# Attention and MLP in one kernel: another order of the pieces, and DMA transposes of exp(C) from batch 2 on

## The chip, the cores and the metric

The kernel runs on one core of one Trainium2 chip. The metric is the device time of a run in microseconds, and less is better. TensorE is PE, VectorE is DVE, ScalarE is ACT, GpSimd is POOL and SyncE is SP. PEld is PE's loading of weights.

## The reference

The program is a Nystrom attention followed by a layer with silu. It has 8 batches, 8 heads, 576 positions and a head size of 64. The landmarks are means over 18 positions, 32 of them for each head.

```python
q_lm = q.reshape(B, H, m, S // m, D).mean(axis=3)      # m = 32
k_lm = k.reshape(B, H, m, S // m, D).mean(axis=3)
A = sm(q, k_lm); Bm = sm(q_lm, k_lm); C = sm(q_lm, k)  # sm: scaled softmax
Z = Bm.T / (norm1(Bm) * norminf(Bm) + 1e-06)
for _ in range(6):
    Z = 2 * Z - Z @ Bm @ Z
attn = A @ Z @ C @ v
x = attn.transpose(0, 2, 1, 3).reshape(B * S, H * D)   # 4608 x 512
h = x @ w_in                                           # 512 x 2048
out = (h * sigmoid(h)) @ w_out                         # 2048 x 512
```

## The kernel before, in words

All work is written as some 1,540 small pieces. A piece has a name, an engine that may do it (sometimes one of two), a duration that the author assumed, the pieces it depends on, a priority, and the PSUM banks it takes. A planner at the top of the file (class Plan) runs through time with these assumed durations and gives every engine that is free the ready piece of lowest rank. The table ORDER adds a shift to the priority of named pieces (`shift, o.ready = ORDER.get(o.name, (0.0, 0.0))`, L87); its second number holds a piece back until a model time. The result is a fixed list for each engine. On the chip every engine works through its list in that order and waits where a piece's inputs or its buffer aren't ready. So a piece that waits holds up all that stands behind it on its engine.

The name of a piece ends in its batch. The ones that matter here:

- ld1, ld0 and ldv0 to ldv2 load k, q and v of a batch (POOL's DMA queue, with a cast to bf16). wi.. and wo.. load the weights of the two layers. The buffers qk, qT, v, ct, ce and lm have two copies, which even and odd batches use in turn.
- tr and trc (batches 0 and 1) transpose k and q on PE and copy them to qT. From batch 2 on, four DMA transposes on SP do this: xt10 and xt11 for k (head groups 0 and 1), xt00 and xt01 for q (L587).
- lra, lrb, lrc and lrd on DVE add up the landmarks from qT. lra1 takes both groups of k and lra0 both groups of q. ltr1 and ltr0 are PE matmuls with the matrix `fold` that finish them, and lmT copies them out.
- sb, pb, csb, f0, ns and nsd are the softmax of Bm and the iteration for Z: a chain that goes between PE and DVE.
- C and A are the scores. Cx and Ax are their exponentials on ACT (into ce and et). S, Ln, Rs and etn divide A by its sums. exp(C) has to be transposed. Before the change batches below NCT = 4 do that with six PE transposes for each head group (ctm, L825) and one copy out of PSUM (ctc). Later batches do it with one DMA transpose on SP (ct, L837). cv multiplies with v, and wc, zt and m with mc make the matrix m = Z C v w_in.
- h0 to h15, hx0 and hx8 multiply A with m on PE. g0 to g15, gx0 and gx8 apply silu on ACT, into gm and gx. These steps need another ACT table than exp does, and a table load stands at each change.
- The last product is done for pairs of 128-position blocks with seven half-size products instead of eight. ss0 to ss3 on DVE make the sums of blocks of gm. p1 to p7 are the products on PE, 8 matmuls each. c1, u2, c5, c11, c22, c12 and c21 bring them to the output buffer ost (four copies, used in turn) on ACT or DVE, and os stores it through SP's queue. A name such as p1@5120 has the batch in its hundreds (batch 1, second pair). The first pair of all is done plainly (o0 to o3 at 5000 and 5001, and oc).

Transfers of different kinds are kept apart by extra waits. The transposes of q and k of batch b wait until ldv1 of that batch has landed (L582). The loads of batch b + 1 wait for one transpose of batch b, which is the third that the code creates, xt00:

```python
gate = last[b - 1]["xts"][-2:-1] if b > NPE else []     # L1122, NPE = 2
if b - 2 >= NCT:
    gate = gate + last[b - 2]["cts"][:1]
load_qk(b, 100.0 * b - 150, p["qk_read"], gate)
load_v(b, 100.0 * b - 149, [p["cv"]], gate)
```

The code creates the transposes in the order xt10, xt11, xt00, xt01. The order in which SP issues them is the planner's.

PE also has filler matmuls (on the zero tile zer) in the first 45 us, where the planner sees it idle.

## Time and profile before

| | us |
|---|---|
| median of 3 runs | 259.06 (258.79 to 259.65) |
| profiled execution | 259.06 |
| its span | 257.3 |
| PE busy | 241.2 (94%) |
| ACT busy | 180.7 (70%) |
| DVE busy | 171.8 (67%) |
| PE transposes of exp(C), 48 | 3.6 (mean 219 ns) |
| fillers, 95 | 15.9 (mean 299 ns) |
| DMA transposes on SP | 24 of q and k, 8 of exp(C) |

Busy time is the union of an engine's instructions. Matmuls overlap on PE, so a mean of 219 ns for a transpose doesn't say how far apart two of them start. The time of a DMA is in two parts: how long SP or POOL is taken up by issuing it, and how long it is from there until it has landed.

### The profile page before, as it was taken

What the parts mean: (1) busy time and instruction counts of PE and PEld (TensorE: products, weight loads), DVE (VectorE), ACT (ScalarE), POOL (GpSimd) and SP (SyncE); (2) the same over time, 40 slices, a digit from 0 to 9 for tenths busy, and PEclk for the clock granted to TensorE, in tenths of its full rate; (3) what the DMA queues carried; (4) which work ended last, traced back from release to release, by engine and by line L of the source; (5) the groups of instructions that cost most, each with busy time, mean ns of one, the idle gap of its engine ahead of it and who ended that gap; (6) DMA issues with size and microseconds to landing.
All of it is one profiled execution on the core that took longest, in us unless ns stands there. A gap on an engine that the chain in (4) does not pass through costs nothing.

```text
span 257.3 us, 7005 instructions
## 1 busy us (share of the span) xinstructions
PE 241.2 (94%) x2737; PEld 169.6 (66%) x2737; DVE 171.8 (67%) x433; ACT 180.7 (70%) x428; POOL 37.8 (15%) x64
## 2 busy tenths in 40 slices
PE   7999998999979789999979999999999999999990
PEld 5875655646758445567866655788785585788870
DVE  2378736597958776939979769199995654157520
ACT  2697799689852899997449989678679957721210
POOL 8446621004004003100310040000000000000000
PEclk9999999999999999999999999999999999999997
DMA  5999999999999998996796989974341203033332
GB/s 96 212 195 201 203 207 208 202 154 179 216 179 139 234 171 149 204 175 148 131 225 157 137 156 222 194 164 111 77 105 32 54 3 82 0 85 82 85 103 61
DMA packets 57201, 36.90 MB, mean 143 GB/s; under 512 B 38112, under 2 KB 48608, under 8 KB 57168
## 3 DMA queue, kind: packets, MB, share of 16 engines
q0 software_dynamic: 15296, 18.42, 43.2%
q1 hardware_dynamic: 41536, 17.74, 32.8%
q8 instruction: 21, 0.34, 0.6%
q10 hardware_dynamic: 336, 0.30, 0.4%
q14 instruction: 12, 0.10, 0.1%
HBM read 36.70 MB, written 9.44 MB: 179 GB/s over the span
## 4 chain that ended last, share of the span: by engine, by line
issue 40%; PE 30%; DMA 13%; ACT 4%; SPq 4%; DVE 4%; POOL 3%; POOLq 0%; DVEq 0%; ACTq 0%
PE ps L388 30%; DMA v<-in_v_dram 5%; DMA qT<-qk 3%; DMA w_in_sb<-in_moe_w_in_dram 3%; ACT gm L937 2%; DMA out_dram<-ost 2%; SPq L587 2%; SPq L1002 2%; DVE m L400 1%; POOL qk L446 1%; POOL qk L440 1%; PE ps L825 1%; POOL v L453 1%; DVE st L735 1%; DVE red L623 1%
## 5 line engine op out<-in xcount | busy, mean ns | idle before, releaser
L388 PE MATMUL ps<-etn,m 128*128 128x512 bf16 (+1 forms) x512 | 69.6, 286 | 0.7 <-DVE m L400 0.7
L937 ACT ACTIVATE gm<-ps 128x512 f16<-128x512 f32 x128 | 66.1, 682 | 3.0 <-PE ps L388 2.9
L388 PEld LDWEIGHTS <-gm 128*128 128x128 f16 x512 | 48.4, 98 | 12.7 <-issue 4.5
L388 PE MATMUL ps<-w_out_sb,gm 128*128 128x256 f16 (+1 forms) x392 | 53.9, 281 | 0.9 <-ACT et L765 0.8
L398 ACT COPY ost<-ps 128x256 f32<-128x256 f32 (+1 forms) x59 | 22.5, 386 | 41.2 <-PE ps L388 32.7
L388 PEld LDWEIGHTS <-m 128*128 128x128 bf16 x512 | 31.9, 98 | 26.2 <-issue 5.4
L388 PEld LDWEIGHTS <-ss 128*128 128x128 f16 x408 | 39.5, 98 | 6.9 <-issue 0.2
L1060 DVE TENSOR_TENSOR ost<-ost,ps 128x256 f32<-128x256 f32 x51 | 21.3, 419 | 25.5 <-PE ps L388 10.2
L388 PE MATMUL ps<-wt,ss 128*128 128x256 f16 x272 | 33.9, 273 | 0.0
L735 DVE SCALAR_TENSOR_TENSOR st<-st,ps 128x320 bf16<-128x320 bf16 (+3 forms) x54 | 21.7, 407 | 10.9 <-PE ps L388 10.6
L400 DVE CAST m<-ps 128x512 bf16<-128x512 f32 x32 | 20.9, 687 | 4.1 <-PE ps L388 3.4
L398 ACT CAST m<-ps 128x512 bf16<-128x512 f32 x32 | 17.6, 617 | 2.9 <-PE ps L388 2.8
L453 POOL DMA_DIRECT2D v<-in_v_dram x24 | 14.0, 591 | 26.1 <-PE ps L388 22.0
L388 PE MATMUL ps<-w_out_sb,ss 128*128 128x256 f16 x136 | 17.6, 272 | 0.0
L388 PE MATMUL ps<-zer 128*128 128x256 bf16 x95 | 15.9, 299 | 1.1 <-DVE zer L480 1.1
L446 POOL DMA_DIRECT2D qk<-in_k_dram x7 | 5.0, 716 | 77.1 <-DMA qT<-qk 56.6
L810 ACT ACTIVATE ce<-ps 128x288 bf16<-128x288 f32 x32 | 12.7, 412 | 4.9 <-PE ps L388 4.9
L388 PE MATMUL ps<-wt,gm 128*128 128x256 f16 x120 | 15.6, 273 | 0.0
L1002 POOL DMA_DIRECT2D out_dram<-ost x1 | 0.5, 527 | 97.1 <-DVE ost L1060 97.1
L388 PE MATMUL ps<-st 128*128 128x160 bf16 (+1 forms) x96 | 14.6, 225 | 0.1
L400 DVE COPY ost<-ps 128x256 f32<-128x256 f32 (+1 forms) x11 | 4.9, 448 | 12.2 <-PE ps L388 12.1
L765 ACT ACTIVATE et<-ps 128x288 bf16<-128x288 f32 x32 | 10.8, 418 | 2.5 <-PE ps L388 2.5
(91 smaller groups left out, 331.3 us busy)
## 6 DMA issues: line engine op xcount, KB each, us to landing
out_dram<-ost SPq DMA_DIRECT2D x137, 64.0 KB, 2.1
v<-in_v_dram POOLq DMA_DIRECT2D x24, 192.0 KB, 11.7
qk<-in_k_dram POOLq DMA_DIRECT2D x7, 576.0 KB, 6.2
qk<-in_q_dram POOLq DMA_DIRECT2D x7, 576.0 KB, 9.0
w_out_sb<-in_moe_w_out_dram POOLq DMA_DIRECT2D x4, 512.0 KB, 10.5
w_in_sb<-in_moe_w_in_dram POOLq DMA_DIRECT2D x4, 256.0 KB, 9.3
w_in_sb<-in_moe_w_in_dram POOLq DMA_DIRECT2D x8, 128.0 KB, 7.5
qk<-in_k_dram POOLq DMA_DIRECT2D x2, 288.0 KB, 4.9
```

The source lines that it names most:

```text
L388: nc.tensor.matmul(out=out_ap, lhsT=lhsT, rhs=rhs, start=start, stop=stop, skip_group_check=True)
L398: nc.scalar.copy(out=out, in_=in_)
L400: nc.vector.tensor_copy(out=out, in_=in_)
L446: lambda e, t=t, src=src: nc.gpsimd.dma_start(out=qk_r[b % 2][:, t].rearrange("p g j d -> p g (j d)"), in_=src[b].rearrange("(g h) (l j) d ...
L453: lambda e, a=a: nc.gpsimd.dma_start(out=v_r[b % 2][a * L:(a + 1) * L, :, :], in_=v[b].rearrange("h (l a x) d -> a l h (x d)", l=L, a=VA)[ ...
L587: lambda e, t=t, g=g: nc.sync.dma_start_transpose(out=qT[:, t, g], in_=qk[:, t, g].rearrange("p j d -> p (j d)")),
L735: nc.vector.scalar_tensor_tensor(out=s2[:, g0:g1, lo:SW], in0=s[:, g0:g1, lo:SW], scalar=2.0, in1=ps[:, 0:NG * SW].rearrange("p (g x) -> p ...
L765: lambda e, g=g, et=et, c=c: nc.scalar.activation(out=et[:, c], in_=bank(me["A"], 2 * g + c)[:, 0:HS], func=AF.Exp, scale=sc / J),
L810: nc.scalar.activation(out=ce[:, :, 0:VP].rearrange("p (i c) (a l) -> p c a i l", c=2, a=VA)[:, c], in_=bank(me["C"], 2 * g + c)[:, 0:HS]. ...
L937: lambda e, dc=dc, cell=cell: nc.scalar.activation(out=gm[:, dc, :], in_=bank(cell["o"]), func=AF.Silu),
L1002: {"SP": nc.sync, "ACT": nc.scalar, "POOL": nc.gpsimd}[e].dma_start(out=out[b * S:(b + 1) * S, cols].rearrange("(l j) n -> j l n", j=J)[j] ...
L1060: nc.vector.tensor_tensor(out=out_, in0=x, in1=y, op=OP.add)
```

## The change

NCT becomes 2, so batches 2 and 3 also transpose exp(C) by DMA on SP. By L1123 the loads of batches 4 and 5 then wait for the first such transpose of the batch two before as well. The table ORDER is another one, with 77 entries in place of 46. The first loads are written as a list LOADS with one priority each, and load_qk can load k or q alone; the list names the loads in the sequence they had.

```diff
 ORDER = {
-    "ld11.0": (-7.7871, 0), "lms006.0": (45.257, 0), "nsd11.0": (-1.7367, 0),
...
-    "n1.6": (-1615.8, 0), "Ln10.6": (-887.04, 0), "h6.6": (115.44, 0), "p2@5740.0": (1.5405, 0),
+    "ld00.0": (-5.0016, 0), "tr014.0": (-121.13, 0), "stf0.0": (177.85, 0), "ns40.0": (105.91, 0),
...
+    "xt00.2": (-7.9428, 0),
+    "xt01.2": (-1.9866, 0), "ldv1.3": (-3099.2, 0), "S01.2": (2357.7, 0), "etn0.2": (3457.6, 0),
...
+    "C.3": (0.55052, 79.781),
...
+    "p3@5740.0": (334.88, 0),
 }
...
-    NCT = 4
+    NCT = 2
     XLAG = 3.0
+    LOADS = "k1 q1 v0 w0 w1 w2 w3 o0 o1 o2 o3 v1".split()
...
-    def load_qk(b, prio, deps=(), after=()):
-        for t, src in ((1, k), (0, q)):
+    def load_qk(b, prio, deps=(), after=(), ts=(1, 0)):
+        for t in ts:
+            src = k if t else q
...
-    load_qk(1, -95)
-    load_v(0, -90)
-    for f in range(4):
-        load_w_in(f, -80 + f)
-    for c in range(4):
-        load_w_out(c, -50 + c)
-    load_v(1, -40)
+    for i, x in enumerate(LOADS):
+        p, n = -95 + i, int(x[1])
+        {"k": lambda: load_qk(n, p, ts=(1,)), "q": lambda: load_qk(n, p, ts=(0,)),
+         "v": lambda: load_v(n, p), "w": lambda: load_w_in(n, p),
+         "o": lambda: load_w_out(n, p)}[x[0]]()
```

What the new table does to the lists can be read by putting the two programs' instructions side by side. PE has 2,700 matmuls in place of 2,737: 24 PE transposes fewer and 82 fillers in place of 95. SP has four more DMA transposes of exp(C). On SP the parts that stand otherwise, up to batch 3:

```
before: os@5000 xt10.2 xt11.2 xt00.2 xt01.2 os@5001 os@5020 xt10.3 xt11.3 os@5021 xt00.3 xt01.3 os@5100
after:  os@5000 os@5001 xt00.2 xt01.2 xt10.2 xt11.2 os@5020 os@5021 xt10.3 xt11.3 xt00.3 xt01.3 ct0.2 ct1.2
```

On POOL's queue, for batches 2 and 3:

```
before: ld1.2 ld0.2 ldv0.2 ldv1.2 ldv2.2 ldv1.3 ld1.3 ld0.3 ldv0.3 ldv2.3
after:  ld1.2 ld0.2 ldv1.2 ldv2.2 ldv1.3 ld1.3 ld0.3 ldv0.3 ldv2.3 ldv0.2
```

On PE, around the landmarks and scores of batch 2:

```
before: ... h13.1 ltr1.2 h14.1 h15.1 p6@5020 ltr0.2 hx8.1 p1@5100 sb.2 p7@5020 p2@5100 C.2 p4@5020 p5@5100 A.2
after:  ... h15.1 ltr1.2 hx8.1 h4.1 h10.1 ltr0.2 p1@5100 p1@5120 sb.2 p5@5100 C.2 p6@5100 p6@5120 A.2
```

From batch 4 on, SP takes a batch's transposes in these orders: xt01 xt00 xt10 xt11 (batch 4), xt00 xt01 xt10 xt11 (batch 5), xt00 then ct0.5 and ct1.5 and then xt10 xt01 xt11 (batch 6), xt01 xt00 xt10 xt11 (batch 7). Before, all were xt10 xt11 xt00 xt01.

## The prediction

> **What bounds the kernel now.** I read the page's busy times, the table of 10 us windows, the waits of PE, then the SP, POOL and ACT timelines between 50 and 75 us. Piece names are those of the code (kind, tensor and head group, batch); a piece is found in the timeline by its tiles and place in order.

> ```profile
> span 257.3 us, 7005 instructions
> PE 241.2 (94%) x2737; PEld 169.6 (66%) x2737; DVE 171.8 (67%) x433; ACT 180.7 (70%) x428; POOL 37.8 (15%) x64
> ```

> ```profile
> 70.00:80.00 10.00, 8.22 (x99) 6.97 (x97) 6.83 (x17) 4.74 (x12) 0.03 (x1) 1.00 1.11 173
> 80.00:90.00 10.00, 8.40 (x124) 6.05 (x121) 8.15 (x27) 6.40 (x23) 3.12 (x5) 1.00 1.02 199
> ...
> 150.00:160.00 10.00, 10.00 (x89) 5.41 (x87) 8.73 (x19) 9.27 (x21) 3.14 (x5) 1.00 0.95 172
> ```

> PE is the bound: 94% of the span, and full in most windows after 30 us. So PE work removed, or a PE wait added, reaches the end nearly one for one. The first 30 us are held by the loads instead. What idles PE in the middle is little:

> ```profile
> PE ps L388 <- ACT ct L398: 1.7, 1, 1.7
> PE ps L388 <- ACT lmT L398: 1.4, 1, 1.4
> ```

> The first is at 71.9 us. ACT stood 2.2 us before c1@5120, whose ost buffer still had a store in flight; the ct copy behind it kept a PSUM bank. The second, at 129.9 us, is the same kind: c5@5300 waits for a store, and lmT0.5 stands behind it.

> The transfers decide those stores, and the rest of this prediction:

> ```profile
> 51.03 6.74 SPq L587 DMA_TRANSPOSE qT<-qk  x4
> 57.87 8.51 SPq L1002 DMA_DIRECT2D out_dram<-ost  x8
> 66.55 5.93 SPq L587 DMA_TRANSPOSE qT<-qk  x2
> ```
> ```profile
> 58.89 0.58 POOL L453 DMA_DIRECT2D v<-in_v_dram  x1 [17.61 <-PE ps L388]
> 59.46 0.71 POOL L446 DMA_DIRECT2D qk<-in_k_dram  x1
> 60.16 0.72 POOL L446 DMA_DIRECT2D qk<-in_q_dram  x1
> 60.88 1.18 POOL L453 DMA_DIRECT2D v<-in_v_dram  x2
> ```

> SP transposes batch 2 with four DMA transposes from 51.03 us; the qT view gives them 3.3 to 3.7 us to landing. Batch 3's loads start at 58.89, about 0.6 us after xt00.2, the third of the four, landed (54.94 + 3.4 = 58.3); the code gates them on that one. By the time these loads move data, all four are through. For the two transposes at 66.55 and 68.70, issued while these loads ran, the same view answers:

> ```profile
> DMA to landing us min/median/max: 5.8/6.4/7.0
> ```

> and the second took 3.8 us to issue instead of 1.3. In 64 to 66 us the DMA engines carry 214 GB/s at a share over 1: full. A transpose that meets loads lands about when the loads are done (the last landed at 72.5).

> [...] SP's transposes and stores slow down when POOL's loads run (3.4 to 7.0 us); what share a transpose keeps, no row shows alone. [...] Here that is 12 transposes in 0.83 us and copies of 0.56 (DVE) or 0.83 us (ACT).

> **The change, part by part.**

> (a) PE transposes out. For batches 2 and 3, 24 matmuls: the block of 12 at 87.56 us lasts 0.83 us, less the 0.22 us of one, over 11 steps, 55 ns each: **-1.3 us** of PE. Three DVE copies (1.7 us) and one ACT copy (0.8) go too.

> (b) DMA in their place: ct0 and ct1 of batches 2 and 3, 1.27 us of SP each, 2.5 us to landing (rows at 119.56 and 140.50). Between C.2 and cv0.2 the new order has seven product pieces of 0.87 us: covered, priced at 0 (up to +1 if SP is late). With NCT at 2, loads of batches 4 and 5 also wait for ct0.2 and ct0.3; batch 4's loads went out at 79.97, and in the new order ct0.2 lands near there: 0.

> (c) The load list names the same loads in the same sequence; within w_in two pieces swap (wi3a before wi2b1, about 1 us). m2.0 also moves behind h0, h1, h2, h4: 0, bounds -0.5 and +0.5.

> (d) The first silu phase. Before, g0 starts at 30.07: lmT0.1 (26.34), pb.1 (27.61), mc20.0, a table load of 1.28. After, ltr0.1 precedes m0 and m1, and ACT does no mc20 before the table load. m1 still waits for its weights (about 25.1), so sb.1 is at 25.6, pb.1 after mc10 and mc11 at 26.7, g0 at 28.2. The 18 silu steps of 0.48 us end near 37.7, with gx8 among them, where before 17 ended at 39.0. PE reaches o0@5000 at 37.0, having left A.1, p1@5020 and ns50.1 (1.5 us) for later: equal to 38.5, against 41.08. **-2.5 us**; the batch 1 copies of m give 0.3 back.

> (e) Batch 2's transposes, the decisive step. SP's order is now xt00, xt01, xt10, xt11 (before: xt10, xt11, xt00, xt01). The gate is unchanged: batch 3's loads wait for xt00.2, now the **first**. ldv0.2 also moves behind them. xt00.2 goes out at about 51 us (t0; it needs ldv1.2, which lands at 50 to 51 as before, and both 5000 stores stand before it on SP). It lands at t0+3.7, POOL starts 0.6 later, and data move about 1.2 us after that: t0+5.5. xt10.2 is issued at about t0+3.9 and xt11.2 at t0+5.3, so nearly all of both, 2 x 0.29 MB, meets 1.92 MB of loads. 2.5 MB at about 0.21 MB/us is 12 us: everything is in by t0+18.

> Who waits: lra1.2 on DVE needs xt10 and xt11, and lra0.2 stands behind it; their chain of 1.7 us (0.69, 0.42, 0.29, 0.29) feeds ltr1.2 on PE. Behind ltr1.2 stand hx8, h4 and h10 of batch 1, and all later sums and products need g4 and g10. PE comes to ltr1.2 at about 61.0 us: before, it was at 61.12 with p4, p6 and p7@5020 (2.6 us) still undone, so 2.7 us ahead. Unhindered, xt11.2 lands at t0+8.6 = 59.6 and ltr1.2 waits 0.5. At the other end it lands with the last load, 69.5: 71.4. I take **67.5**: the transposes get some share during the v loads. Then ltr1.2 runs at 69.4, and the lead of 2.7 has become 69.4 - 61.1 - 2.6 = **5.7 us lost**. Ends of this step: -2.3 and +7.7.

> SP's own queue: the second store of 5020 stands behind these transposes and batch 3's behind the store; they land near 75 us, before the DVE's lra1.3 in the shifted order.

> (f) Batches 2 and 3 after that. The wait at 71.9 goes: no ct copy, and c1@5120 stands ahead of the table load: -1.7. What is late next: DVE takes both pairs' sums (8 x 0.6 us) before the batch chain, so p6@5100, f0.2, ns00.2 and ns20.2 wait 0.5 to 1 us each: +1.7, less up to 1 for what other waits cover.

> (g) The wait at 129.9: lmT0.5 stands ahead of c5@5300, and p7@5300 ahead of p5: -1.4 (to 0 if pb.5, now behind c5, is late instead).

> (h) Batch 6: SP's order is xt00.6, ct0.5, ct1.5, then the other three; batch 7's loads wait for the first two only. Three transposes meet the loads and land some 12 us later; ltr1.6 is needed about then: +1.5 (0 to +4). Batch 4's xt11 meets them in part: 0 to +1.

> Sum: 5.7 - 1.3 - 1.7 + 1.7 - 1.4 + 1.5 = **+4.5** (the -2.5 of (d) is inside the 5.7). The profiled execution took 259.06 us, its span 257.3 and 1.8 around it; that is also the median. 259.06 + 4.5 = 263.5. The tail has the same products and the last stores on the same queues: 0.

> **The rivals.**

> Main, 263.5, with worse forms up to 268: 0.74.

> The collision costs little. Transposes are issued before the loads move[...]: the four before took only 6.7 us to issue. Then (e) is -2.3 and the sum -2.3 - 1.3 - 1.7 + 1.7 - 1.4 + 1 = -4: **255.0**, faster. One mechanism decides: when xt11.2 lands. From the sum, the gain is gone when ltr1.2 runs at 64.9, that is when it lands later than about 63 us. For it: no row shows a transpose against k and q loads alone. Against: 7.0 us to landing at 66.55, with only half of the loads left. 0.20.

> Half and half: xt10 gets through before the k load, xt11.2 lands at about 63, and the gain of the shorter PE work is eaten: 259. 0.06.

> That ct isn't moved can't be: the order shows four more DMA transposes and no PE transpose of ce after batch 1.

> **How the numbers follow.** About 0.3% (0.8 us) is what a measurement of this kernel tells from none. Faster 0.20, same 0.06, slower 0.74. The time is the main case's, 263.5. The range 256.0 to 268.0 reaches into the other cases: below is the better part of the 255 case (0.13), above are xt11.2 at its latest with (h) at its worst (0.06). The main case's own range is 260 to 268.

> **What would show it.** In the changed profile: PE with one gap of 5 to 9 us near 61 us before the matmul with fold, DVE's first red of batch 2 released by DMA qT<-qk; the third and fourth qT transposes with 8 to 13 us to landing; g0 at about 28.2; no PE wait on ct after batch 1. Wrong if these transposes land within 5 us: then the time should be near 255, with DVE sums as the next wait. Wrong otherwise if a loss sits after 100 us.

## The result, and the profile after

The changed kernel takes 273.73 us (median of 4 runs, 273.15 to 274.20) against 258.93 us in the same session: 1.0575 times as long, 95% interval 1.0528 to 1.0621. Forecast were 263.5 us and a range of 256 to 268. The direction was right, the size was not: 14.8 us were lost, not 4.5. Below, a median is over all executions of a kernel, and its ratio leaves out those that took over 1.5% more than the fastest of the same kernel.

The head of its page: busy times, and PE's own row and the clock row out of the forty slices of 6.8 us.

```profile
span 272.2 us, 6908 instructions
PE 242.0 (89%) x2700; PEld 169.6 (62%) x2700; DVE 168.8 (62%) x429; ACT 180.9 (66%) x428; POOL 37.8 (14%) x64
...
PE   8998999990589999999999951999999999999990
...
PEclk9999999997599999999999995799999999999998
```

PE is busy as long as before (242.0 us against 241.2), yet the span is 14.9 us longer. The new time is idle time, in two places: slices 10 and 11 (61 to 75 us) and slices 24 and 25 (157 to 170 us). In and behind each hole PEclk falls to 7 and 5 (the first) or to 5 and 7 (the second), where before it was 9 up to the tail (the row of before):

```profile
PEclk9999999999999999999999999999999999999997
```

PE's waits (engine, line, releaser: us in total, times, longest):

```profile
PE ps L403 <- DVE rs L637: 19.0, 2, 9.9
PE ps L403 <- DVE zer L496: 1.1, 1, 1.1
PE ps L403 <- ACT pb L689: 0.9, 1, 0.9
```

Both holes have the same releaser, the last step of the sum of the transposed k (lrd1). The two waits of before, for ct (1.7 us) and lmT (1.4 us), are gone. PE's timeline shows which pieces stood:

```profile
70.85 0.37 PE L403 MATMUL ps<-rs,fold 128*128 128x256 f16 x1 [9.89 <-DVE rs L637]
...
169.41 0.37 PE L403 MATMUL ps<-rs,fold 128*128 128x256 f16 x1 [9.10 <-DVE rs L637]
```

These are ltr1.2 and ltr1.6, the matmuls with fold of batches 2 and 6. The timelines of POOL and SP show what they waited for, here around the first hole:

```profile
54.98 0.58 POOL L469 DMA_DIRECT2D v<-in_v_dram  x1 [16.19 <-DMA qT<-qk]
55.54 0.71 POOL L462 DMA_DIRECT2D qk<-in_k_dram  x1
56.25 0.71 POOL L462 DMA_DIRECT2D qk<-in_q_dram  x1
56.95 1.74 POOL L469 DMA_DIRECT2D v<-in_v_dram  x3
```
```profile
50.96 6.02 SPq L601 DMA_TRANSPOSE qT<-qk  x4
57.07 12.16 SPq L1016 DMA_DIRECT2D out_dram<-ost  x8
```

Batch 3's loads leave at 54.98, 0.6 us after xt00.2, the first transpose of batch 2, has landed (54.40). The view of the tile qT gives the landings of these four:

```profile
DMA to landing us min/median/max: 3.3/3.4/13.5
```

Three get through in 3.4 us; the fourth, xt11.2, issued at 55.36, needs 13.5 and lands at 68.90. Around the second hole it is three of four, at 6.2, 15.3 and 12.6 us (SP's timeline, then the same tile's view):

```profile
145.85 1.29 SPq L601 DMA_TRANSPOSE qT<-qk  x1
147.23 2.59 SPq L851 DMA_TRANSPOSE ct<-ce  x2
149.91 12.86 SPq L601 DMA_TRANSPOSE qT<-qk  x3
```
```profile
DMA to landing us min/median/max: 3.2/9.4/15.3
```

xt11.6 is held on SP's queue until 154.86, takes 7.9 us to issue and lands at 167.46. PE had come to ltr1.6 at 160.3.

### The profile page after: what moved, and what is told of

It reads as the page before. It is cut to its first block, busy times and chain, and to the rows that moved or that the text cites. A ratio compares the mean times of both kernels' runs of the same rounds, so it can differ in the third digit from the quotient of the medians.

```text
span 272.2 us, 6908 instructions
## 1 busy us (share of the span) xinstructions
PE 242.0 (89%) x2700; PEld 169.6 (62%) x2700; DVE 168.8 (62%) x429; ACT 180.9 (66%) x428; POOL 37.8 (14%) x64
## 4 chain that ended last, share of the span: by engine, by line
issue 41%; PE 38%; DMA 12%; POOL 2%; DVE 2%; ACT 2%; SPq 1%; POOLq 0%; DVEq 0%
PE ps L403 37%; DMA qT<-qk 5%; DMA v<-in_v_dram 4%; DMA w_in_sb<-in_moe_w_in_dram 3%; POOL qk L456 1%; DVE m L415 1%; SPq L601 1%; POOL v L469 1%; DVE red L637 1%; POOL qk L462 1%; ACT et L779 0%; ACT m L413 0%; ACT ln L789 0%; DVE st L749 0%; PE ps L839 0%
## 5 line engine op out<-in xcount | busy, mean ns | idle before, releaser
L403 PE MATMUL ps<-etn,m 128*128 128x64 bf16 (+1 forms) x512 | 70.2, 289 | 0.4 <-ACT gm L951 0.4
L951 ACT ACTIVATE gm<-ps 128x512 f16<-128x512 f32 x128 | 66.9, 649 | 3.2 <-PE ps L403 2.9
L637 DVE TENSOR_TENSOR red<-qT 128x1024 f16<-128x1024 bf16 x14 | 9.6, 688 | 27.9 <-DMA qT<-qk 27.8
L403 PE MATMUL ps<-rs,fold 128*128 128x256 f16 x14 | 4.2, 297 | 19.0 <-DVE rs L637 19.0
L413 ACT CAST m<-ps 128x512 bf16<-128x512 f32 x35 | 18.7, 614 | 3.0 <-PE ps L403 3.0
L415 DVE CAST m<-ps 128x512 bf16<-128x512 f32 x29 | 19.0, 685 | 2.4 <-PE ps L403 2.3
L403 PE MATMUL ps<-w_out_sb,ss 128*128 128x256 f16 x136 | 18.5, 281 | 0.0
L403 PEld LDWEIGHTS <-st 128*128 128x128 bf16 x96 | 8.7, 98 | 14.9 <-issue 10.3
L403 PE MATMUL ps<-wt,gm 128*128 128x256 f16 x120 | 16.5, 282 | 0.0
L403 PE MATMUL ps<-zer 128*128 128x256 bf16 x82 | 14.3, 307 | 1.1 <-DVE zer L496 1.1
## 6 DMA issues: line engine op xcount, KB each, us to landing
w_in_sb<-in_moe_w_in_dram POOLq DMA_DIRECT2D x4, 256.0 KB, 9.7
```

Source lines behind the costliest of these rows:

```text
L403: nc.tensor.matmul(out=out_ap, lhsT=lhsT, rhs=rhs, start=start, stop=stop, skip_group_check=True)
L413: nc.scalar.copy(out=out, in_=in_)
L415: nc.vector.tensor_copy(out=out, in_=in_)
L637: lambda e: nc.vector.tensor_tensor(out=o_, in0=a_, in1=b_, op=OP.add),
L951: lambda e, dc=dc, cell=cell: nc.scalar.activation(out=gm[:, dc, :], in_=bank(cell["o"]), func=AF.Silu),
```

## The experiments

The theory, T1: transposes of q and k that are issued after the one that gates the next batch's loads meet these loads; ltr waits for them; PE's clock is halved behind each hole (PEclk 0.50 from 64.84 to 75.08 us and from 163.83 to 174.07). Rivals: exp(C) transposed by DMA is what costs (T2); the new order costs by waits of its own (T3); the clock falls for a reason of its own (T4). A helper that runs after the planning puts a batch's loads behind given transposes and leaves every engine's own sequence as it is (shortened):

```
order = P.run()
def behind(b, order, xs):
    lds = [x for x in order if x[0].name in (ld1.b, ld0.b, ldv0.b, ...)]
    for x in lds:
        x[0].after = list(x[0].after) + [o for o in xs if o not in x[0].after]
    # then the loads move behind the last of xs in the emitted order
```

**Batch 7's loads behind all of batch 6's transposes.**

```
+order = behind(7, order, last[6]["xts"])
```

> The second half alone: only batch 7's loads wait for all transposes of batch 6. T1: the gap near 61 us stays (9.9 us), the one near 160 goes: 273.7 - 9.1 - 2.2 = 262.4. If batch 7's loads, now some 8 us later, are late themselves, a new PE wait shows after 175 us and the time is over 265.

Measured: 264.57 us, ratio 1.0208 (1.0154 to 1.0262). xt11.6 lands at 158.59, and ltr1.6 runs at 161.54 with no wait:

```profile
PE ps L403 <- DVE rs L637: 10.6, 1, 10.6
PE ps L403 <- ACT gx L974: 1.8, 1, 1.8
```

One of the two waits is left, the one at 61 us; a new one of 1.8 us (h2.5, at 170 us) comes up, for a PSUM bank behind c5@5400, whose ost buffer still has its store in flight. As T1 has it, this collision is worth 9 to 10 us: the hole of 9.1 and its half clock (1.9, below) less the new wait of 1.8 make 9.2.

**Both, and batch 3 alone.** The first two kernels for this did not do what they were to:

```
+order = behind(3, order, last[2]["xts"])   # e1_both and e2_b3
+order = behind(7, order, last[6]["xts"])   # e1_both only
```

> The changed kernel, every engine's order kept, with one thing undone: batch 3's loads wait for all four transposes of batch 2, and batch 7's for all four of batch 6. If the two collisions are the loss (T1), xt11.2 lands near 60 us and xt11.6 near 157, both long PE gaps (9.9 and 9.1 us) go, so do the 2.2 us of half clock behind each, and the time is 273.7 - 9.4 - 9.1 - 4.4 = 251 (249 to 253). If the transposed exp(C) costs (T2) or the new order itself (T3), the gaps go but the time stays above 259. If the clock falls for a reason of its own (T4), it still shows 0.5 in two stretches and the time is about 255.

> The first half of that alone: only batch 3's loads wait for all transposes of batch 2. T1: the gap near 61 us and its half-clock stretch go, the gap before ltr1.6 stays at about 9 us with its stretch: 273.7 - 9.4 - 2.2 = 262. If the two gaps are one cause (the second an echo of the first), both go and it is 251. If lost time is only moved to a later wait, over 268.

Measured: 265.58 and 274.73 us. In this first form the helper added the wait only to loads that it had to move, and batch 3's loads already stood behind the transposes in the emitted order. So e1_both is e3_b7 again and e2_b3 the changed kernel again: the hole at 61 us is there in both. They say nothing on batch 3; as repeats they show the scatter, about 1 us each. With the wait really added:

> The changed kernel, every engine's order kept, with batch 3's loads really waiting for all four transposes of batch 2 (in e1_both and e2_b3 these loads already stood behind the transposes in the emitted order, so the edit found nothing to move and added no wait; those two differ from their parents in nothing for batch 3) and batch 7's for all four of batch 6. T1: xt11.2 lands near 60 us, ltr1.2 runs at about 61.5, no PE gap over 2 us and no half clock behind it: e3_b7's 264.6 - 9.9 - 1.5 = 253 (251 to 256). T3, the new order's own waits: the gap goes but waits of the same size come before 110 us, time 259 to 264.

> The first half of that alone: only batch 3's loads wait for all four transposes of batch 2. T1: the gap at 61 us goes, the one near 160 comes 10 us earlier and keeps its 9 us and its half clock: 273.7 - 11.4 = 262 (260 to 265). Rival: with the work 10 us earlier, batch 7's loads and batch 6's transposes shift alike, so nothing else changes; if instead a transfer fixed in time becomes late (the loads of batches 3 and 4 start 5 us later), the time is over 266.

Measured: both 261.94 us, ratio 1.0100 (1.0041 to 1.0160); batch 3 alone 271.81 us, 1.0473 (1.0404 to 1.0543). All four transposes of batch 2 land in 3.5 us at most (xt11.2 at 58.53), ltr1.2 runs at 60.63, and still only 2 to 3 us are gained, little more than the scatter, where over 11 were expected. PE's waits of e7_both name the reason, and DVE's timeline shows it:

```profile
PE ps L403 <- DVE pbs L708: 6.2, 1, 6.2
```
```profile
68.16 0.22 DVE L699 TENSOR_TENSOR bm<-pb,pbs 128x64 bf16<-128x64 f32 x1
75.34 0.69 DVE L637 TENSOR_TENSOR red<-qT 128x1024 f16<-128x1024 bf16 x1 [6.96 <-DMA qT<-qk]
...
76.86 0.22 DVE L708 TENSOR_REDUCE pbs<-ps 128x2 f32<-128x64 f32 x1
```

DVE stops at lra1.3, the first sum of batch 3, until xt11.3 lands at 75.3; batch 2's chain (n1.2 and what follows) stands behind it in the new order, and PE waits 6.2 us for that chain. In the changed kernel the hole at 61 us covered this wait: DVE comes to lra1.3 at 79.85 there, with its input landed. This is T3, in one place, but its length is once more a collision: xt10.3 and xt11.3, issued at 66.2 and 68.5, take 8.1 and 6.8 us to landing beside the loads of their own batch (7.0 and 5.8 in the kernel before, where DVE stands 2.6 us at lra1.3 and PE doesn't wait for it). How long PE's wait would be without that, no run shows.

**The third transpose as gate**, as the kernel before has it:

```
+order = behind(3, order, last[2]["xts"][:1])   # xt10.2, issued third
+order = behind(7, order, last[6]["xts"])
```

> As e7_both, but batch 3's loads wait only for xt10.2, the third transpose issued, as in the kernel before. T1 in the form of the prediction: the loads' first data move about 1.8 us after a landing, when the fourth is nearly through, so xt11.2 still lands by 61.5 and the time is that of e7_both or up to 1 us less (loads 1.4 us earlier). If the fourth alone can be caught as well, it lands after 65 us, a gap of 5 us or more returns and the time is 259 or more.

Measured: 262.05 us, ratio 1.0109 (1.0052 to 1.0165), the same as e7_both. The transpose still in flight when the loads are released gets through (all four take 3.4 us at most); it is the first as gate that is harmful.

**The collision alone, in the kernel before.** The gate becomes xt10.2, which is issued first there:

```
+    for o, e, t, end, switch in order:
+        if o.name in ("ld1.3", "ld0.3", "ldv0.3", "ldv1.3", "ldv2.3"):
+            o.after = last[2]["xts"][:1]
```

> The kernel before, every engine's order kept, with only this added: batch 3's loads wait for the first transpose of batch 2 (xt10.2) in place of the third. T1: the loads start near 55 us, the fourth transpose xt01.2 meets them and lands near 67 us (before: 59.6), lra0.2 stands on it, and ltr0.2 on PE, which ran at 63.0, waits to about 69.5: a gap of 6 us and some half clock behind it, less the 1.7 of the wait at 71.9: 259.5 + 6 = 265.5 (262 to 268). If the collision needs the new order to hurt (T3), within 1 us of before.

Measured: 268.77 us against 258.91, ratio 1.0359 (1.0288 to 1.0430): 9.9 us, some 3 more than expected but of the expected kind. PE's timeline shows ltr0.2, as the last transpose there is one of q (14.6 us to landing):

```profile
72.75 0.37 PE L388 MATMUL ps<-rs,fold 128*128 128x256 f16 x1 [10.14 <-DVE rs L623]
```

One changed gate makes a hole of 10.1 us, with the clock at half from 68.0 to 78.2, in a kernel whose order is otherwise untouched. The collision needs nothing of the new order but the gate.

**The clock.** 75 matmuls of zeros ahead of ltr1.2 and of ltr1.6, then 92 and 82:

```
 def ltr(e, t=t):
     ps = bank(me["ltr", t])
+    if t and b in (2, 6):
+        for _ in range(75):               # e16_fill: 92 if b == 2 else 82
+            mm(ps[:, 0:256], zer[:, 0:128], zer)
```

> The changed kernel with 75 matmuls of zeros (256 columns, about 0.11 us each, 8 us) put on PE just ahead of the fold matmul ltr1.2 and of ltr1.6, so that PE is busy in both gaps; nothing else is touched. If the half clock comes from PE's idling (T1), the granted clock stays at 1.0 behind both gaps and the time falls by about 2 x 2.2 us to 269.3. If it has another cause (T4), the clock falls as before and the time is 273.7 or a little more.

> As e6_fill, with 92 and 82 matmuls of zeros in place of 75: the wait left behind them is about 1.2 us in the first gap and 0.6 in the second. If the half clock comes from PE's idling over some 2 to 4 us (T1), it stays away in both, and the time is 273.7 - 2 x 2 = 269.7 (269 to 271). If it comes from something else, a stretch at 0.5 shows all the same and the time is 273 or more.

Measured: 273.37 us (ratio 1.0520) and 272.10 us (1.0512, interval 1.0458 to 1.0566). In e6_fill 3.0 us of idling were left ahead of ltr1.2 and the clock still fell, to 0.50 for 3.4 us. In e16_fill it holds to the tail:

```profile
PEclk9999999999999999999999999999999999999996
```

For these two holes T4 falls. In the traces, the stretch from ltr1.2 to C.2 took 7.48 us in the changed kernel and 5.87 in e16_fill, that from ltr1.6 to p1@5400 5.23 and 3.36: the half clock costs 1.6 and 1.9 us. But the median fell by only 1.6 us, about the width of its interval to one side, where 4 were expected; ltr1.2 ran 1.0 us later in the profiled execution, and the rest is not assigned. So the 3.5 us are what the two stretches show; the whole run has given back 1.6 of them.

**exp(C) by DMA or by PE.** One constant in each kernel, and the planner then orders the pieces anew:

```
-    NCT = 2
+    NCT = 4        # e10_nct4: on e7_both
-    NCT = 4
+    NCT = 2        # e13_before_ct: on the kernel before
```

> e7_both with exp(C) of batches 2 and 3 transposed on PE again (NCT = 4; the planner then puts out its own order with the same table ORDER, so pieces from 70 us on stand differently). If the DMA form of these four transposes costs (T2), this is faster than e7_both by 2 us or more: 260 or less. If not (T1, T3), the same DVE wait for xt10.3 and xt11.3 shows at 71 us and PE has 1.3 us more work: 261 to 265.

> The kernel before with only the transposes of exp(C) for batches 2 and 3 given to DMA (NCT = 2; the planner orders the pieces from 70 us on anew with the table ORDER of before, SP runs ct0.2 and ct1.2 between xt10.3 and xt11.3). T1: no collision of batch 2, so no gap at 61 us; PE is rid of 1.3 us and of the wait of 1.7 at 71.9 us, and cv0.2 may wait for ct up to 2 us: 256 to 260. If DMA in place of PE is what costs (T2): over 262, with PE waits that name ct or that sit between C.2 and cv0.2.

Measured: 268.66 us, ratio 1.0394 (1.0329 to 1.0459), and 268.39 us, 1.0375 (1.0307 to 1.0443). Each half alone is some 10 us slower than before. With PE transposes the changed order has the same wait (6.3 us), now for the ct copy behind lra1.3 on DVE, and more of them after 130 us. With DMA transposes, the order that the old table now gives puts ct0.2 and ct1.2 between batch 3's transposes on SP, and the first store of batch 2 behind ct0.4 and ct1.4: it leaves at 124.64, where before stores left at 117.43, and from 131 us PE waits for ost buffers:

```profile
PE ps L388 <- ACT ost L398: 3.8, 3, 2.0
PE ps L388 <- ACT lmT L398: 1.9, 1, 1.9
```

Both expectations were missed. T2 is neither shown nor excluded by them: the planner's orders differ from 70 us on. What they show is that table and NCT belong together, so neither can be priced alone. The bound on both together is e7_both: with its DMA transposes it is 3.0 us above the kernel before.

**Undoing the order's own wait.** Moves on e7_both, by a helper that puts named pieces behind another (in e12_pe, e14_best and all that take over its moves, ns30.2 is also given another PSUM bank; "..." marks names left out):

```
+put("lra1.3 lrb1.3 lrc1.3 lrd1.3", "stf0.2")                 # e11_dve

+put("lra1.3 lrb1.3", "etn1.2"); put("lrc1.3 lrd1.3", "nsd10.2")   # e12_pe
+put("lra0.3 lrb0.3 lrc0.3 lrd0.3", "c11@5120")
+put("ltr1.3", "p2@5120"); put("lmT1.3", "c5@5120")
+put("cv0.2 ... ltr0.3 lmT0.3 wc.2 sb.3", "p4@5120")

+put("lra1.3 lrb1.3 lrc1.3 lrd1.3", "nsd20.2")                # e14_best
+put("ltr1.3 lmT1.3", "ns30.2"); put("lra0.3 ... lrd0.3", "c11@5120")
+put("p3@5120", "p4@5120"); put("cv0.2 ... sb.3", "p3@5120")
+order = behind(4, order, last[2]["cts"])
```

> e7_both with one thing moved: on DVE the four sums lra1.3, lrb1.3, lrc1.3 and lrd1.3 of batch 3, which stand ahead of batch 2's chain (wrc.2 to stf0.2) and wait for transposes that land at 75.3 us, go behind stf0.2. In e7_both PE stood 6.2 us before S00.2 for that. If this order is what kept the gain from showing (T3, in this one place), S00.2 runs at about 71; then ltr1.3, fifth piece after it, waits for lrd1.3 (75.3 + 1.7) until 77.3, and c22@5100 behind lra0.3: PE arrives 3 us earlier than in e7_both: 262 - 3 = 259 (257 to 261). If batch 3's transposes bound this stretch whatever stands where, nothing: 262.

> e7_both with every step that needs batch 3's transposes or the transposed exp(C) of batch 2 moved behind work that doesn't: on DVE lra1.3 to lrd1.3 behind etn1.2 and nsd10.2, lra0.3 to lrd0.3 behind c11@5120; on PE ltr1.3 behind p2@5120, cv0.2 and ltr0.3 behind p4@5120 (the loads of v for batch 4 and sb.3 follow cv0.2). T1 with T3: PE has 8 us of work from 71 to 79, the gap of 6.2 us and the 1.5 us of half clock behind it go, up to 1 us of wait for ct1.2 at 79.9 comes: 262 - 6.7 = 255.3 (253 to 258), under the kernel before. If the stretch is bound by the transfers, a PE wait of 4 us or more shows between 71 and 82 all the same and the time is 258 or more.

> e7_both with the stretch from 70 to 84 us ordered so that nothing stands behind batch 3's transposes or ct1.2 before they land: on DVE lra1.3 to lrd1.3 behind nsd20.2 and lra0.3 to lrd0.3 behind c11@5120; on PE ltr1.3 behind ns30.2, p3@5120 behind p4@5120, then cv0.2 and ltr0.3; and batch 4's loads wait for both DMA transposes of exp(C) of batch 2, not the first alone (in e12_pe ct1.2 met these loads and landed at 82.3). T1 with T3: no PE gap over 1.5 us between 62 and 84 us; e12_pe's 260 less its 3.8 us gap: 256 (254.5 to 257.5), faster than before by 1%. If transfers bind the stretch, a gap over 2.5 us stays and it is 258.5 or more.

Measured: 260.90 us (ratio 1.0112), 260.00 us (1.0059, interval 1.0024 to 1.0094) and 263.33 us (1.0124, interval 1.0051 to 1.0198; single executions from 260.1 to 265.8). The wait moved each time. In e11_dve it is ltr1.3 that stands 5.3 us; in e12_pe it is ns20.2, because nsd10.2 stood behind lrb1.3. In e14_best it is gone, and PE's timeline has only small pieces of it:

```profile
74.58 0.31 PE L403 MATMUL ps<-st 128*128 128x160 bf16 x2 [0.69 <-DVE st L749]
...
77.35 0.27 PE L403 MATMUL ps<-rs,fold 128*128 128x256 f16 x1 [0.58 <-DVE rs L637]
...
79.97 0.53 PE L403 MATMUL ps<-v,ct 96*64 96x128 bf16 x12 [0.38 <-DMA ct<-ce]
...
81.21 0.53 PE L403 MATMUL ps<-v,ct 96*64 96x128 bf16 x12 [0.71 <-DMA ct<-ce]
```

But the lead does not last. The profiled execution of e14_best, which is its slowest (265.8 us), starts p2@5120 at 75.6, 9.5 us ahead of e7_both; A.3 at 82.5, 4.9 ahead; h0.3 at 105.6, 1.5 ahead; then h2.3 waits 2.6 us, and the clock is at half for 17 us in three stretches. e18_nofill, below, loses the lead in an ordinary execution too: A.3 at 82.7, h0.3 at 107.6. So something else holds the stretch from 80 to 110 us.

**The same moves with the collisions left in.**

> The changed kernel with only these moves on DVE and PE, and no load made to wait longer: both collisions are as in the changed kernel. If the collision at 61 us hides the waits of the order behind it (the two are in parallel, not in series), the time is that of the changed kernel, 273.7 (272 to 275). If they add up, 6 us less: 267.5.

Measured: 278.04 us, ratio 1.0745 (1.0678 to 1.0812), slower than the changed kernel by 4. Neither expectation. ltr1.2 ran 1.3 us later than in the changed kernel in the profiled execution, p2@5120 0.4 us later, A.3 3.7 us later: what is lost is lost between the last two. A reading that fits is that with PE late by the hole nothing of batch 3 is late any more, so that the moved pieces only come later than need be; no run tests it.

**A last attempt**, e14_best with lra1.4 behind two copies that held a bank, and that with 24 matmuls of zeros:

```
+put("lra1.4", "mc30.3")                                 # e18_nofill, e17_fill
+mm(bank(me["cv0"])[:, 256:512], zer[:, 0:128], zer)     # e17_fill: 4 + 8 at cv0.2
+mm(ps[:, 0:256], zer[:, 0:128], zer)                    # e17_fill: 12 at h2.5
```

> e14_best with one more move on DVE: lra1.4, which waited for xt11.4 ahead of two copies of m that hold the PSUM bank of h2.3, goes behind them (mc20.3, mc30.3). The PE gap of 2.6 us at 106.6 us and the half-clock window behind it go; the stretch at half clock from 82 us and the one at 171 us stay: 263.3 - 2.6 - 1.5 = 259.2 (257.5 to 261.5).

> e18_nofill with 24 matmuls of zeros more (256 columns, 0.11 us each): 4 ahead of cv0.2, 8 between its two halves, where PE waits for ct1.2, and 12 ahead of h2.5, where PE waits 2 us for a bank. [...] no stretch at half clock is left before the tail, and the kernel with more work is faster: 259.2 less about half of 10.2 and 3.4 us at half speed, each less what is idle anyway: 255.5 (254 to 257.5), under the kernel before. If the clock has another cause, the stretches stay and the time is that of e18_nofill or up to 1 us more.

Measured: 262.78 us, ratio 1.0131 (1.0078 to 1.0184), and 263.97 us, 1.0214 (1.0164 to 1.0264). In the profiled execution e17_fill's clock was at half for only 3.4 us ahead of the tail (6.8 us in e18_nofill), and yet it was not faster. What binds 80 to 110 us after the moves stays open; the clock is not all of it. No version beat the kernel before.

## Why the prediction missed

**(a), (b), (d), (g) held.** No PE transpose of ce after batch 1, and no PE wait on ct. g0 runs at 28.1 (said: 28.2), the silu steps end at 38.0 (37.7), PE reaches o0@5000 at 36.6 (37.0). The wait at 129.9 is gone. (c) missed that the table also changes the order of batch 0's four loads; g0 at 28.1 shows no loss from it.

**(e) held in kind and nearly in size.** xt11.2 lands at 68.9 (said: 67.5) and ltr1.2 runs at 70.85 (69.4): 7.1 us lost there, where 5.7 were said. Off was only that xt10.2 got through; one late transpose is enough.

**(h) is the term that failed.** It was put at +1.5, at most +4; the hole is 9.1 us, and e3_b7 shows that the collision makes it. It is the same collision as (e), but it was not worked out with the same care: "t0+18" of step (e), from xt00.6 at 145.85, gives 163.9 for the landing, 165.8 for ltr1.6, 5.5 us after PE comes to it at 160.3. Two ct transposes ahead on SP, and loads that start before two of the three transposes are even issued, made it 167.5. The prediction named its own refutation: a loss that sits after 100 us.

**The clock was left out.** The halved clock behind the two holes (0.50 for 10.24 us each) costs 1.6 and 1.9 us in the stretches behind them; in both holes it begins 3.5 to 3.9 us after PE stops. The prediction had no term for it. The kernel before has a lower clock in its tail alone (PEclk 0.77 from 250 us on, where PE is busy for 0.37 us of 7.3); its longest wait of PE, 1.7 us at 71.9, left the clock at 1.00. In the runs of this case, the holes of 9 and 10 us carry the halved clock as part of their cost.

**(f) was wrong underneath, unseen.** The prediction saw, under (e), that batch 3's transposes land near 75 us and held that this is before lra1.3 is reached. It is so only because of the hole: without it, DVE is there at 68.4, and PE waits 6.2 us. So the rival's 255.0 was wrong as well: with both gates mended the kernel takes 262, not 255. Of the 14.8 us, batch 6's collision with its clock is 9 to 10, batch 2's only 2 to 3 on top of the wait it covers, and 3.0 remain with the new order and its DMA transposes, which no run tells apart. Each of these has some 1.5 us of scatter to either side. e12_pe may get back half of the 3.0 (1.5 us, within that scatter).

The terms do not close exactly: predicted +4.5, and +7.6 for (h), +3.5 for the clock, +1.4 for (e) give 17.0 against 14.8; the 2.2 us are not assigned. With the 1.6 us that the whole run gained when the clock held, in place of 3.5, the sum is 15.1.

## What to carry to other kernels

A gate on the first of several transposes does not guard the others: ask of every wait which transfer it names, and which are still queued behind that one. When one instance of a mechanism is worked out with care, work out every other instance in the program in the same way, with its own start and its own need. And a wait that a larger wait covers costs nothing until the larger one is mended, so a rival's time has to be walked through as carefully as the main case.

## What the runs showed of the hardware

Beside loads in packets of 2.2 KB, the transpose in flight (xt11.2) moved 0.02 MB/us. In the 5 us from 60 us of the changed kernel, the DMA view has, by queue (packets, MB, share of 16 engines):

```profile
q0 software_dynamic: 413, 0.91, 95.2%
q1 hardware_dynamic: 414, 0.11, 16.4%
```

There are as many packets of one queue as of the other, 2.2 KB of a load (q0) on average and 256 bytes of a transpose (q1): 0.11 MB in 5 us, or 0.02 MB/us, where transposes alone (52 to 56 us: 3061 packets, 0.77 MB) moved 0.19. In each single us from 59 to 69 the two counts differ by 4 at most, at 77 to 202 packets of q0.
